# The first chunk of a gated recurrence: whole loads of k, q and v, f by halves of heads, one more transpose by DMA, and a new order of the program

## The chip, the cores and the metric

The kernel runs on one core of a Trainium2 chip. The metric is device time in microseconds for one launch. Three runs of the kernel before took 181.29, 182.45 and 182.78 us; the median, 182.45 us, is the time to compare with.

## What is computed

The reference is a linear recurrence with a gate for each key channel, followed by a two-layer network with a leaky ReLU. There are 4 batches, 8 heads, 768 tokens and 48 channels for each head; the network is 384 to 2048 to 384.

```python
f = 1.0 / (1.0 + np.exp(-f_logit))
for t in range(S):
    state = f[:, :, t, :, None] * state + np.einsum('bhd,bhe->bhde', k[:, :, t], v[:, :, t])
    y[:, :, t] = np.einsum('bhd,bhde->bhe', q[:, :, t], state)
x = y.transpose(0, 2, 1, 3).reshape(B * S, H * D)
h = x @ w_in
out = np.maximum(0.01 * h, h) @ w_out
```

## The kernel before, in words

**Units.** The 768 tokens are cut into 6 chunks of 128. One chunk of one batch is a unit: 24 units, numbered so that units 0 to 3 are the first chunk of the four batches (the first quad), 4 to 7 the second chunk, and so on. Two neighbouring units are a pair `m`.

**A unit from the second chunk on.** f, k, q and v are loaded with tokens on partitions (`load_part`, L171, 192 KB each, runs of 192 B). ScalarE makes log(1 + exp(-f)) (`gate_exp`, `gate_ln`), TensorE sums it over tokens with a triangular matrix (`gate_pe`, L328), and ScalarE makes the decays from it (`decay_em`, `decay_a`). `k_scale` and `q_scale` multiply k and q by them. They are turned, so that channels lie on partitions, by TensorE (`turn_pe`) or for a pair at once by DMA (`turn2_dma`, L376). `score_pe` makes the scores, `mask` cuts them to the lower triangle, `mix_pe` (L418) makes the 128x384 result from the scores and the state, and `state_pe`, `state_dve`, `state_pool` carry the state on. `y_out` puts the result into SBUF as bf16, and it is turned once more for the network: by TensorE (`x_pe`, L453, three transposes, and `x_out`), or for a pair by one DMA on SP's queue (`x2_dma`, L380), for the pairs that the tuple `X2` (L200) lists.

**The network.** `up` (L462) makes two of the 16 blocks of hidden channels for a pair, 6 products of 256 columns; `up_act` is its leaky ReLU on ScalarE. `down` (L484) is one half of the second layer for a unit, 8 products of 384 columns. `put` and `out_dma` store the result. A pair has 8 `up`; units 4 and 5 have forms of their own for one unit (`up1`). The weights are loaded and cast to bf16 by DMAs of GpSimd's queue: `load_w_in` in two halves (half 0 serves groups 0 to 3 of `up`, half 1 groups 4 to 7), `load_w_out` in four parts.

**The first quad** has a form of its own (functions with `q_`), since all four units start from a state of zero. f of all four is loaded into one tile `fq` with 32 partitions for each batch, each holding four neighbouring tokens, so that a run is 768 B; k and q (`kq`, `qq`) likewise, but with the batches interleaved on the partitions. One ScalarE instruction then handles half of the heads of all four units (`q_exp_act`, L228, and `q_ln_act`, L231). `q_gate32` (L234) makes the sums over tokens for half of the heads into four banks, one for each batch; `q_decay_b` (L243) makes the decays of a batch, for half of the heads or all, positive sign (`emT`) or negative (`aT`). `q_k_cast`, `q_q_cast` make bf16 of k and q, `q_turn_pe` turns them, `q_mul` (L260) multiplies by the decays. Then come `q_score_pe`, the mask (`q_mask` on VectorE, or an eviction by ScalarE, `q_wf_act`, with `q_mask_pool` on GpSimd), `q_back_pe` and `q_back_out` (k turned back for the state), `state_pe`, `q_mix_pe`, `y_out`, `x_pe` and `x_out`. v of units 0 to 3 comes by four `load_part` and four `cast_v`.

**The order.** Nothing is scheduled by the compiler. The program is a list written out call by call (from L513), and each engine and each DMA queue runs its part of the list in that order; waits follow from which tile or bank is read and written. So a wait of one engine holds back all that stands behind it on that engine. SP's queue issues the loads, stores and transposing DMAs, and holds back everything behind a DMA whose data is not ready. `touch` (L183) is a small copy on GpSimd that waits for a load and so delays the weight loads behind it on the queue. `idle_pe` (L140) issues dummy products on TensorE.

Of the kernel before, what the change touches and what calls it, by code (L numbers as in the profile page):

```python
# [9 lines left out]
FP32 = mybir.dt.float32  # L10
# [6 lines left out]
def kernel(  # L17
# [50 lines left out]
    def load_quad(eng, t, src, b, h):  # L68
        rows = slice(32 * b, 32 * b + 32) if t is fq else slice(b, None, 4)
        eng.dma_start(out=t[rows, h, :, :].rearrange("p h j d -> p h (j d)"),  # L70
                      in_=src[b, h, 0:C, :].rearrange("h (t j) d -> t h (j d)", j=4))

    quads = {"f": (fq, f_logit), "k": (kq, k), "q": (qq, q)}

    def first_load(eng, name, b, hh=None):
        load_quad(eng, quads[name][0], quads[name][1], b, slice(0, H) if hh is None else slice(4 * hh, 4 * hh + 4))
# [7 lines left out]
    first_load(nc.sync, "k", 1)  # L84
    first_load(nc.sync, "k", 2)
    first_load(nc.sync, "k", 3)
    first_load(nc.sync, "q", 0)
    first_load(nc.sync, "q", 1)
    first_load(nc.sync, "q", 2)
    first_load(nc.sync, "q", 3)  # L90
# [80 lines left out]
    def load_part(u, name, src):  # L171
        c, b = units[u]
        t = raws[f"{name}_raw"][u % R_RAW]
        nc.sync.dma_start(out=t, in_=src[b, :, c * C:(c + 1) * C, :].rearrange("h t d -> t h d"))
        raw.setdefault(u, {})[name] = t
# [24 lines left out]
    X2 = (9, 10, 11)  # L200
# [23 lines left out]
    emT, aT = wide(gTs[GBUFS - 1]), wide(gTs[GBUFS - 2])  # L224
    kTq = [const.tile([128, 2, 4, 128], BF16, name=f"kTq{i}", tag=f"kTq{i}") for i in range(2)]
# [287 lines left out]
    q_exp_act(0)  # L513
    q_ln_act(0)
    load_part(0, "v", v)
    q_exp_act(1)
    load_part(1, "v", v)
    idle_pe(24, 7)
    q_gate32(0, 0, 1, 2, 3)
    touch('k')  # L520
    q_k_cast(V, 0)
    q_ln_act(1)
    q_k_cast(G, 1)
    q_turn_pe(khq, 0, 4)
    load_part(2, "v", v)
    q_decay_b(0, aT, -1.0, 0, 0)
    q_gate32(1, 0, 1, 2, 3)
    q_decay_b(1, emT, 1.0, 1, 0)
    load_w_in(0)
    q_decay_b(0, emT, 1.0, 0, 0)  # L530
    q_decay_b(2, emT, 1.0, 2, 0)
    q_turn_pe(khq, 1, 5)
    q_k_mul(0, 1, 0, 4)
    q_decay_b(1, aT, -1.0, 1, 0)
    load_w_in(1)
    q_decay_b(2, aT, -1.0, 2, 1)
    q_k_mul(0, 0, 0, 4)
    q_decay_b(1, emT, 1.0, 1, 1)
    load_part(3, "v", v)
    q_q_cast(V, 1)  # L540
    q_decay_b(3, emT, 1.0, 3, 1)
    q_decay_b(0, emT, 1.0, 0, 1)
    q_q_cast(V, 0)
    idle_pe(6, 7)
    q_turn_pe(qhq, 1, 6)
    q_decay_b(0, aT, -1.0, 0, 1)
    load_part(4, "f", f_logit)
    cast_v(G, 0)
    q_decay_b(1, aT, -1.0, 1, 1)
    q_k_mul(1, 0, 0, 5)  # L550
    q_turn_pe(qhq, 0, 7)
    q_decay_b(2, aT, -1.0, 2, 0)
    q_k_mul(1, 1, 0, 5)
    q_decay_b(2, emT, 1.0, 2, 1)
    q_q_mul(1, 0, 0, 6)
    q_decay_b(3, aT, -1.0, 3, 1)
    cast_v(G, 1)
    idle_pe(1, 1)
    q_back_pe(1, 0)
    q_q_mul(1, 1, 0, 6)  # L560
    q_decay_b(3, aT, -1.0, 3, 0)
    q_back_pe(0, 1)
    q_q_mul(0, 0, 0, 7)
    q_decay_b(3, emT, 1.0, 3, 0)
    q_back_out(A, 0, 1)
    q_q_mul(0, 1, 0, 7)
    idle_pe(2, 2)
    q_score_pe(1, 0, 2, 3)
    q_back_out(V, 1, 0)
    q_q_mul(1, 0, 1, 6)  # L570
    q_score_pe(0, 0, 1, 0)
    q_wf_act(1, 0, 1, 3)
    q_mask(1, 0, 0, 2)
    state_pe(1, 3)
    q_wf_act(0, 0, 1, 0)
    q_mask_pool(1, 0, 1)
    q_mask(0, 0, 0, 1)
    state_pe(0, 2)
    q_state_dve(0)
    q_mask_pool(0, 0, 1)  # L580
    q_k_mul(0, 0, 1, 4)
    q_mix_pe(1, 0)
    q_state_pool(0)
    load_part(4, "k", k)
    q_mix_pe(0, 1)
    q_k_mul(1, 0, 1, 5)
    y_out(A, 1, 0)
    q_state_dve(1)
    y_out(A, 0, 1)
    idle_pe(3, 2)  # L590
    x_pe(1, 2)
    q_k_mul(1, 1, 1, 5)
    x_pe(0, 0)
    q_state_pool(1)
    x_out(A, 1, 2)
    q_q_mul(0, 1, 1, 7)
    x_out(A, 0, 0)
    q_q_mul(1, 1, 1, 6)
    q_q_mul(0, 0, 1, 7)
    idle_pe(5, 1)  # L600
    q_score_pe(1, 1, 1, 3)
    q_k_mul(0, 1, 1, 4)
    up(0, 2, 5)
    q_mask(1, 1, 0, 1)
    q_wf_act(1, 1, 1, 3)
    q_back_pe(3, 2)
    up(0, 1, 6)
    up_act(0, 2, 5)
    q_mask_pool(1, 1, 1)
    q_back_out(V, 3, 2)  # L610
    up(0, 0, 0)
    up_act(0, 1, 6)
    q_score_pe(0, 1, 7, 4)
    up_act(0, 0, 0)
    up(0, 3, 3)
    q_mask(0, 1, 0, 7)
    q_wf_act(0, 1, 1, 4)
    load_part(4, "q", q)
    cast_v(G, 2)
    q_back_pe(2, 1)  # L620
    up_act(0, 3, 3)
    load_w_out(0)
    q_back_out(V, 2, 1)
    idle_pe(1, 0)
    up(0, 4, 5)
    load_part(4, "v", v)
    cast_v(V, 3)
    q_mask_pool(0, 1, 1)
    state_pe(2, 2)
    up(0, 5, 6)  # L630
    up_act(0, 4, 5)
    load_w_out(1)
# [756 lines left out]
```

## Time and profile before

| quantity | value |
|---|---|
| median of three runs | 182.45 us |
| the profiled execution | 182.43 us, span 180.7 us |
| TensorE busy | 171.3 us, 95% of the span |
| ScalarE busy | 123.4 us, 68% |
| VectorE busy | 87.0 us, 48% |
| GpSimd busy | 54.8 us, 30% |
| DMA moved | 31.31 MB, mean 173 GB/s |
| last product ends, last eviction ends | 177.50 us, 177.85 us |

PE in the profile is TensorE's matrix product, PEld its loading of the stationary operand (which overlaps), DVE is VectorE, ACT ScalarE, POOL GpSimd, SP SyncE. Times in a timeline are from the start of the span: start, length, engine, line of the kernel, operation, output and input, count, and in brackets how long the engine stood idle before it and who ended the wait. Helpers hide the caller: `move` (L148, L150) stands for all copies. The matrix unit can be called busy while its clock is halved; the column PEclk of the table by stretches shows the granted clock.

### The profile page before, as it was taken

How to read it: one execution, taken by the hardware profiler on the slowest of the kernel's cores; microseconds unless marked ns; L12 is line 12 of the kernel's file. 1: busy time of each engine (PE TensorE's matmuls, PEld its weight loads, DVE VectorE, ACT ScalarE, POOL GpSimd, SP SyncE). 2: the span in 40 equal slices, each digit the busy share in tenths (PEclk: the TensorE clock that was granted, in tenths of full speed). 3: DMA queues.
4: the chain of work that ended last, by engine and by line, in shares of the span. 5: the costliest groups of instructions: out<-in, count | busy, mean ns of one | idle time of the engine just before them, and what ended most of it. 6: DMA issues, size and time to landing. Idle time of an engine off the chain costs nothing.

```text
span 180.7 us, 4845 instructions
## 1 busy us (share of the span) xinstructions
PE 171.3 (95%) x1912; PEld 137.7 (76%) x1912; DVE 87.0 (48%) x203; ACT 123.4 (68%) x268; POOL 54.8 (30%) x108
## 2 busy tenths in 40 slices
PE   7597899999999999979999999999999999999992
PEld 5375699776788889669778788788785696897872
DVE  7249954044765978176467365670750254100000
ACT  2577689546888998758779669578796382583711
POOL 3074453114455646330421804250532300000000
PEclk9969999999999999999999999999999999999999
DMA  5999999979988999999999999998999962050102
GB/s 151 303 221 192 211 173 228 210 157 202 219 188 180 193 173 199 169 209 254 163 192 218 185 206 144 249 186 172 234 207 205 201 180 44 5 131 0 44 25 109
DMA packets 112582, 31.31 MB, mean 173 GB/s; under 512 B 105008, under 2 KB 111280, under 8 KB 112560
## 3 DMA queue, kind: packets, MB, share of 16 engines
q1 hardware_dynamic: 110640, 27.47, 79.7%
q0 software_dynamic: 1376, 3.15, 9.5%
q10 hardware_dynamic: 544, 0.39, 0.8%
q8 instruction: 15, 0.25, 0.6%
q14 instruction: 7, 0.06, 0.1%
HBM read 25.17 MB, written 4.72 MB: 165 GB/s over the span
## 4 chain that ended last, share of the span: by engine, by line
PE 54%; ACT 0%; issue 0%
PE ps L466 24%; PE ps L486 22%; PE ps L404 2%; PE ps L425 2%; PE ps L491 1%; PE ps L422 1%; PE ps L332 1%; PE ps L456 1%; PE ps L433 1%; PE ps L335 0%; ACT osb L148 0%
## 5 line engine op out<-in xcount | busy, mean ns | idle before, releaser
L486 PE MATMUL ps<-w_out_b,gT 128*128 128x384 bf16 x368 | 65.9, 326 | 0.0
L466 PE MATMUL ps<-xT,w_in 128*128 128x256 bf16 x528 | 64.5, 273 | 1.0 <-DVE xT L150 1.0
L471 ACT ACTIVATE gT<-ps 128x512 bf16<-128x512 f32 x88 | 51.7, 601 | 15.0 <-PE ps L466 12.9
L466 PEld LDWEIGHTS <-w_in 128*128 128x128 bf16 x528 | 56.0, 114 | 3.0 <-issue 1.1
L486 PEld LDWEIGHTS <-gT 128*128 128x128 bf16 x368 | 34.5, 98 | 19.8
L415 DVE TENSOR_TENSOR wm<-ps,ut 128x512 bf16<-128x512 f32 x40 | 25.2, 683 | 13.2 <-PE ps L404 11.6
L148 ACT COPY osb<-ps 128x384 f32<-128x384 f32 (+1 forms) x24 | 11.2, 466 | 21.2 <-PE ps L486 17.3
L316 POOL CAST sb<-sf 64x192 bf16<-64x192 f32 x40 | 14.6, 364 | 22.4 <-PE ps L422 18.9
L358 POOL TENSOR_TENSOR kqh<-q_raw,a_t 128x384 bf16<-128x384 f32 x11 | 10.1, 920 | 20.1 <-ACT a_end L344 6.8
L150 DVE CAST xn<-ps 128x384 bf16<-128x384 f32 x15 | 8.3, 556 | 7.6 <-PE ps L425 4.5
L354 POOL TENSOR_TENSOR kqh<-k_raw,em_t 128x384 bf16<-128x384 f32 x7 | 6.4, 918 | 17.6 <-ACT em_t L339 13.3
L354 DVE TENSOR_TENSOR kqh<-k_raw,em_t 128x384 bf16<-128x384 f32 x13 | 8.6, 658 | 6.6 <-ACT em_t L339 6.3
L339 ACT ACTIVATE em_t<-ps 128x384 bf16<-128x384 f32 x20 | 10.0, 498 | 2.0 <-PE ps L335 1.9
L323 ACT ACTIVATE f_raw<-f_raw 128x384 f32<-128x384 f32 x20 | 10.6, 530 | 1.0 <-DMA f_raw<-in_f_logit_dram 1.0
L150 POOL CAST v_b<-v_raw 128x384 bf16<-128x384 f32 x11 | 6.5, 588 | 15.8 <-DMA v_raw<-in_v_dram 15.8
L326 ACT ACTIVATE lf<-f_raw 128x384 bf16<-128x384 f32 x20 | 10.5, 526 | 0.3
L142 PE MATMUL ps<-fill 128*128 128x256 bf16 x46 | 9.3, 364 | 1.3 <-DVE fill L107 1.3
L342 ACT ACTIVATE a_t<-ps 128x384 bf16<-128x384 f32 x20 | 9.9, 495 | 0.8 <-PE ps L335 0.5
L358 DVE TENSOR_TENSOR kqh<-q_raw,a_t 128x384 bf16<-128x384 f32 x9 | 5.8, 644 | 7.2 <-ACT a_t L342 6.8
L150 DVE CAST v_b<-v_raw 128x384 bf16<-128x384 f32 x13 | 6.5, 503 | 5.3 <-DMA v_raw<-in_v_dram 5.2
L447 POOL TENSOR_TENSOR sf<-sf,a_end 128x192 f32<-128x192 f32 x16 | 8.8, 549 | 0.4
L441 DVE TENSOR_TENSOR sf<-sf,ps 64x192 f32<-64x192 f32 x16 | 5.5, 343 | 5.2 <-PE ps L433 1.8
(83 smaller groups left out, 192.6 us busy)
## 6 DMA issues: line engine op xcount, KB each, us to landing
v_raw<-in_v_dram SPq DMA_DIRECT2D x24, 192.0 KB, 4.4
out_dram<-osb SPq DMA_DIRECT2D x23, 192.0 KB, 3.2
f_raw<-in_f_logit_dram SPq DMA_DIRECT2D x20, 192.0 KB, 4.3
k_raw<-in_k_dram SPq DMA_DIRECT2D x20, 192.0 KB, 4.3
q_raw<-in_q_dram SPq DMA_DIRECT2D x20, 192.0 KB, 4.4
w_in<-in_moe_w_in_dram POOLq DMA_DIRECT2D x2, 768.0 KB, 10.8
w_out_b<-in_moe_w_out_dram POOLq DMA_DIRECT2D x4, 384.0 KB, 6.7
kq<-in_k_dram SPq DMA_DIRECT2D x4, 192.0 KB, 4.8
```

Source lines behind the costliest of these rows:

```text
L148: eng.copy(out=out, in_=in_)
L150: eng.tensor_copy(out=out, in_=in_)
L316: nc.gpsimd.tensor_copy(out=state_b[b][r, :, e * D:(e + 1) * D], in_=state_f[b][r])
L323: nc.scalar.activation(raw[u]["f"], raw[u]["f"], AF.Exp, scale=-1.0)
L326: nc.scalar.activation(lfs[u % R_LF][:, :, 0:D], raw[u]["f"], AF.Ln, bias=1.0)
L339: nc.scalar.activation(em_ts[u % R_EM], bank(bk)[:, 0:H * D], AF.Exp, scale=1.0)
L354: eng.tensor_mul(khs[u % R_KQS][:, :, 0:D], raw[u]["k"], em_ts[u % R_EM])
L358: eng.tensor_mul(qhs[u % R_KQS][:, :, 0:D], r["q"], a_ts[u % R_EM])
L415: nc.vector.tensor_mul(wms[e][u % R_WM], bank(bk).rearrange("p (i n) -> p i n", i=P2), ut[:, None, :].to_broadcast([128, P2, 128]))
L466: nc.tensor.matmul(bank(bk)[:, i * 256:(i + 1) * 256].rearrange("p (a n) -> p a n", a=2), w_in_p[ff // 8][:, kk, ff // 4 % 2, :, ff % 4], ...
L471: nc.scalar.activation(gTs[m % GBUFS][:, 2 * g:2 * g + 2].rearrange("p f a n -> p (f a n)"), bank(bk), AF.Prelu, alpha=0.01)
L486: nc.tensor.matmul(bank(bk)[:, 0:KD], g_part(u)[:, ff, :], w_out_b[:, ff, :], start=(ff == 0), stop=(ff == NF - 1))
```

## The change

- f of the first quad is loaded in eight DMAs, the first half of the heads of all four batches ahead of the second half; four on SP's queue, four on ScalarE's.
- k, q and v of the first quad are loaded by one DMA each (`load_all`), with the layout that k and q had. v gets that layout too. It lies in `vq`, and is cast to bf16 as `vqb` by `q_v_cast`. TensorE then puts the tokens of a batch on partitions: `q_pick` multiplies by a selection matrix `pick` (four products of 384 columns for each unit), and `q_v_out` evicts the result as `v_b`. The matrix is set up once, by GpSimd and VectorE. The three tiles lie in buffers of the network that are not in use yet.
- `touch` waits for q instead of k, so that the weights are loaded after q; the second half of `w_in` is now loaded first.
- x of units 16 and 17 (pair 8) is turned by DMA: `X2` is (8, 9, 10, 11).
- The list of calls is new as a whole. Exp and ln of unit 4 now stand among the evictions of the first quad; all four units of the quad stand ahead of the first `up`, but for some products of 2 and 3; the dummy products are placed anew (42 instead of 46); the pairs' `up` and `down` come in another order, as do loads, stores and the choice of engine for copies.

The diff, without most of the new list:

```diff
+    def load_all(t, src):
+        nc.sync.dma_start(out=t.rearrange("p h j d -> p h (j d)"),
+                          in_=src[:, :, 0:C, :].rearrange("b h (t j) d -> t b h (j d)", j=4))
-    first_load(nc.scalar, "f", 2)
-    first_load(nc.sync, "f", 0)
-    first_load(nc.sync, "f", 1)
-    first_load(nc.scalar, "f", 3)
-    first_load(nc.sync, "k", 0)
...
-    first_load(nc.sync, "q", 3)
+    first_load(nc.scalar, "f", 2, 0)
+    first_load(nc.sync, "f", 0, 0)
+    first_load(nc.sync, "f", 1, 0)
+    first_load(nc.scalar, "f", 3, 0)
+    first_load(nc.sync, "f", 0, 1)
+    first_load(nc.scalar, "f", 2, 1)
+    first_load(nc.sync, "f", 1, 1)
+    first_load(nc.scalar, "f", 3, 1)
+    load_all(kq, k)
     nc.scalar.preload_act_table_set("natural_log_exp_and_others")
+    load_all(qq, q)
-    X2 = (9, 10, 11)
+    X2 = (8, 9, 10, 11)
+    pick = spare[:, 0:2048].rearrange("p (b i t j) -> p b i t j", b=B, i=4, j=4)
+    nc.gpsimd.memset(pick, 0.0)
+    for i in range(4):
+        nc.vector.tensor_copy(out=pick[:, :, i, :, i], in_=ident.rearrange("p (t b) -> p b t", b=B))
+    def q_v_cast(eng, hh):
+        move(eng, vqb[:, 4 * hh:4 * hh + 4], vq[:, 4 * hh:4 * hh + 4])
+    def q_pick(b, bk):
+        for i in range(4):
+            nc.tensor.matmul(bank(bk)[:, 0:H * D].rearrange("p (h d) -> p h d", h=H),
+                             pick[:, b, i].rearrange("p t j -> p (t j)"), vqb[:, :, i, :], start=(i == 0), stop=(i == 3))
+    def q_v_out(eng, b, bk):
+        move(eng, v_bs[b].rearrange("p h d -> p (h d)"), bank(bk)[:, 0:H * D])
```

The new list up to the first `up`, by engine (calls of one engine in their order; a number ahead of `x` counts equal calls):

```
SyncE    f 0 and 1 (two halves each), k, q, v; then load_part 4 f, k, q, v; 5 f
ScalarE  q_exp_act 0, q_ln_act 0, q_exp_act 1, q_ln_act 1,
         q_decay_b: aT of 0 (half); gate products of half 1 follow it; then aT 1, emT 1, emT 0, aT 1, emT 1, emT 0 (halves), emT 3, emT 2 (whole),
         q_q_cast 1, aT 2 (whole), aT 0 (half), q_back_out 1, q_back_out 0, aT 3 (whole), q_wf_act 0 0, q_wf_act 1 0,
         q_v_out 1, gate_exp 4, q_v_out 2, gate_ln 4, q_v_out 0, q_wf_act 1 1, q_back_out 3, y_out 1, q_wf_act 0 1,
         y_out 0, decay_a 4, x_out 1, x_out 0
VectorE  q_k_cast 0, 3 x q_k_mul, q_q_cast 0, 3 x q_k_mul, 4 x q_q_mul, q_v_cast 0, q_k_mul, 4 x q_q_mul, q_k_mul,
         q_mask 0 0, q_mask 1 0, q_state_dve 1, q_mask 1 1, q_back_out 2, q_mask 0 1, q_state_dve 0, q_state_dve 2
TensorE  24 x dummy, q_gate32 0, 5 x dummy, q_gate32 1, q_turn_pe k 0, k 1, 9 x dummy, q_turn_pe q 0, q_back_pe 1, q_turn_pe q 1,
         q_back_pe 0, dummy, q_score_pe 0 0, 1 0, q_pick 1, 2, 0, state_pe 1, q_score_pe 1 1, q_back_pe 3, q_score_pe 0 1,
         q_mix_pe 1, state_pe 0, q_back_pe 2, gate_pe 4, q_mix_pe 0, q_pick 3, x_pe 1, state_pe 2, x_pe 0, dummy, q_mix_pe 2, dummy, up(0, 6)
GpSimd   q_k_cast 1, touch q, load_w_in 1, load_w_in 0, q_v_cast 1, q_mask_pool 0 0, 1 0, 1 1, q_state_pool 1, q_mask_pool 0 1, load_w_out 1, 0
```

Behind it on TensorE stand `q_mix_pe(3)`, `state_pe(3)`, `x_pe(2)`, `up(0, 5)`, `up(0, 7)`, `x_pe(3)`, `up(0, 4)`, one dummy and the `up` of pair 1. Further on, around the place at 78 us, the new list has:

```diff
+    cast_v(V, 12)
...
+    x_out(V, 8, 5)
...
+    k_scale(V, 12)
...
+    x_out(V, 9, 0)
...
+    up(4, 7, 1)
```

and for pair 8 `y_out(A, 16, 0)`, `load_part(21, "f", f_logit)`, `x2_dma(8)`, five `up` of pair 7 and three `down`, then `up(8, 0, 5)`.

More of the change, by code (lines that the diff above doesn't have):

```diff
@@ L603 @@
[L603 to L626, printed above, removed]
@@ new lines @@
+    q_v_out(A, 2, 7)
+    state_pe(1, 6)
+    gate_ln(4)
+    q_score_pe(1, 1, 1, 5)
+    q_mask(1, 0, 0, 2)
+    q_v_out(A, 0, 3)
+    q_back_pe(3, 4)
+    q_score_pe(0, 1, 7, 0)
+    q_state_dve(1)
+    q_wf_act(1, 1, 1, 5)
+    q_mix_pe(1, 2)
+    q_back_out(A, 3, 4)
+    state_pe(0, 3)
+    q_mask(1, 1, 0, 1)
+    q_back_pe(2, 5)
+    q_mask_pool(1, 1, 1)
+    gate_pe(4, 6)
+    y_out(A, 1, 2)
+    q_mix_pe(0, 4)
+    q_back_out(V, 2, 5)
+    q_wf_act(0, 1, 1, 0)
+    q_state_pool(1)
+    q_pick(3, 1)
@@ L1167 @@
[L1167 to L1172 removed]
+    score1_pe(4, 2, 6)
+    gate_ln(6)
+    load_part(7, "q", q)
+    put(V, 3, 3)
+    turn_pe(5, 5)
+    mask(4, 0, 2)
+    down(0, 1, 4)
+    turn_q(A, 5, 5)
+    load_part(7, "v", v)
+    turn_k(V, 5, 5)
+    mask(4, 1, 6)
+    gate_pe(6, 7)
+    load_part(8, "f", f_logit)
+    score1_pe(5, 0, 3)
+    put(A, 0, 4)
+    cast_v(V, 6)
+    decay_em(6, 7)
+    mix_pe(4, 2)
+    mask(5, 1, 3)
@@ new lines @@
+    decay_a(6, 7)
+    down(1, 1, 1)
+    load_part(8, "k", k)
+    k_scale(G, 6)
+    y_out(A, 4, 2)
+    mask(5, 0, 0)
+    gate_exp(7)
+    q_scale(G, 6)
+    load_part(8, "q", q)
+    state_pe(5, 5)
+    gate_ln(7)
+    x_pe(4, 6)
+    put(V, 1, 1)
+    state_pe(6, 4)
+    mix_pe(5, 7)
+    x_out(A, 4, 6)
+    state_pool(4)
+    state_dve(5)
+    gate_pe(7, 3)
+    load_part(8, "v", v)
+    turn_pe(6, 2)
+    y_out(A, 5, 7)
+    state_dve(6)
+    decay_em(7, 3)
+    up1(4, 2, 0)
+    decay_a(7, 3)
```

1447 lines of the change are left out of this document (695 added, 752 removed).

## The prediction

> **What bounds the kernel now.** I read the page's head first (busy time, and TensorE's busy tenths in 40 slices of 4.5 us), then TensorE's own waits, and last the start of the timeline engine by engine.
>
> ```profile
> span 180.7 us, 4845 instructions
> ...
> PE 171.3 (95%) x1912; PEld 137.7 (76%) x1912; DVE 87.0 (48%) x203; ACT 123.4 (68%) x268; POOL 54.8 (30%) x108
> ...
> PE   7597899999999999979999999999999999999992
> ```
>
> TensorE's waits from 30 us on, the whole list:
>
> ```profile
> PE ps L466 <- DVE xT L150: 1.0, 1, 1.0
> ```
>
> So TensorE is the bound from the sixth slice on (22.6 us), with one hole of 1.0 us in the eighteenth (near 78 us). Before that it is busy in part only, and in part with dummy products. The end of the kernel is therefore set by three things: when TensorE starts on the dense work (the first `up`), how much useful work is left then, and what holes come later. The tail (last eviction, last store) is the same in both kernels, and I leave it out.
>
> Here is what sets the start now, ScalarE first, then TensorE:
>
> ```profile
> 6.44 0.84 ACT L229 ACTIVATE fq<-fq 128x768 f32<-128x768 f32 x1 [3.39 <-DMA fq<-in_f_logit_dram]
> ...
> 8.92 0.84 ACT L232 ACTIVATE lfq<-fq 128x768 bf16<-128x768 f32 x1
> 9.67 0.37 ACT L245 ACTIVATE gT<-ps 128x256 f32<-128x256 f32 x1
> ...
> 11.16 4.25 ACT L245 ACTIVATE gT<-ps 128x256 f32<-128x256 f32 x15 [1.12 <-PE ps L240]
> 15.14 0.75 ACT L148 COPY kqh<-ps 128x512 bf16<-128x512 bf16 x1
> 15.88 1.10 ACT L281 CAST wm<-ps 128x512 bf16<-128x512 f32 x2
> 18.20 0.86 ACT L148 CAST xn<-ps 128x384 bf16<-128x384 f32 x2 [1.22 <-PE ps L294]
> 19.11 0.86 ACT L148 COPY xT<-ps 128x384 bf16<-128x384 bf16 x2
> ```
>
> ```profile
> 8.21 0.63 PE L240 MATMUL ps<-steps,lfq 32*128 32x128 bf16 x32 [1.74 <-ACT lfq L232]
> ...
> 10.09 1.04 PE L240 MATMUL ps<-steps,lfq 32*128 32x128 bf16 x32
> ...
> 20.98 0.74 PE L466 MATMUL ps<-xT,w_in 128*128 128x256 bf16 x5
> ```
>
> The load of f ends at 6.44; exp and ln of both halves take until 9.76; the gate products of the second half end at 11.13; from there ScalarE's evictions and decays lead, by way of VectorE, to x of units 0 and 1 at 19.97, and the first `up` runs at 20.98.
>
> **The change, part by part.** The sum is made against the profiled execution (182.43 us, span 180.7); the median of the runs is 182.45, the same.
>
> *f in halves.* Four loads become eight of half the size. By these rows the first 393 KB have moved by 3.7 us (151 KB by 3.0, 506 by 4.0), and all 786 KB by 5.0:
>
> ```profile
> 2.00:3.00 1.00, 1.00 (x7) 0.69 (x6) 0.96 (x9) 1.00 (x1) 0.38 (x3) 1.00 0.68 151
> 3.00:4.00 1.00, 1.00 (x6) 0.69 (x5) 0.97 (x10) 0.05 (x1) 0.00 (x0) 1.00 1.07 355
> 4.00:5.00 1.00, 1.00 (x6) 0.74 (x5) 1.00 (x8) 0.00 (x0) 0.00 (x0) 1.00 1.11 290
> ...
> 10.00:11.00 1.00, 0.94 (x33) 0.82 (x32) 0.00 (x0) 0.04 (x1) 1.00 (x3) 0.50 1.32 239
> ```
>
> Exp starts 1.4 after the last byte now, so I let the first half's exp start at 5.1. The ends are 4.4 (the shortest landing in the row below, 3.6 after an issue at 0.8) and 6.44 (no gain). Exp and ln take 3.3 in all as before, so ln of half 1 ends at 8.4.
>
> ```profile
> DMA to landing us min/median/max: 3.6/4.1/5.0
> ```
>
> Issues and landings of q's four loads, for comparison (columns of the first row: least, median and longest issue in ns, first and last issue in us):
>
> ```profile
> L70 SPq DMA_DIRECT2D qq<-in_q_dram x4: 599/606/612, 4.6 to 6.9; - x4
> ...
> DMA to landing us min/median/max: 4.1/4.3/4.5
> ```
>
> The two extra issues on each queue cost at most 0.6 each. They push k's issue and, on ScalarE's queue, the load of the activation table back by up to 1.2; both have until f has landed.
>
> The first decay (0.37) comes ahead of the second gate products and reads the bank that they write, so they start at 8.8. They took 1.04 at a granted clock of 0.50 and the first set 0.63; I take 0.85, which puts their end at 9.7 instead of 11.13. The Trainium skill (TensorE: Matmul & The Clock Gate, Part 1) says that the clock falls to half after an idle window of about 3.4 us; the 0.50 row, after TensorE's pause of 1.74, agrees in kind. The changed order leaves a pause of some 0.4 in that place, so by the rule alone the clock would stay full and the sum below would be 0.2 lower.
>
> *ScalarE from 9.7 to the first `up`.* Ahead of it in ScalarE's new order stand: 7 half decays (4.25 / 15 = 0.28 each, 2.0), 4 whole decays and 4 score evictions of 128x512 (1.10 / 2 = 0.55 each, 4.4), 3 `q_back_out` (0.6 each, between 0.55 and 0.75; 1.8), one cast of q (0.84), 3 `q_v_out`, 2 `y_out` and 2 `x_out` (0.43 each, 3.0), and exp, ln and the decay of unit 4 (about 0.5 each, 1.5). The sum is 13.5, with no wait, so the first `up` runs at 23.2. The check against now: from 11.16 to 19.97 ScalarE has 7.8 of such work and 1.2 of waiting. Every piece is of a kind that the rows above price. Does another engine end later? By the rows below VectorE has, from the first k decays, out at 10.6, to the last mask, 16 products (1.41 / 4 = 0.35), 4 masks (1.27 / 2 = 0.64), a state update (0.73) and three casts or evictions, which I price like a mask: 10.8 in all, to 21.4. That leaves 1.8, and a VectorE late by less is covered.
>
> ```profile
> 14.18 1.41 DVE L263 TENSOR_TENSOR qTq<-ps,gT 128x256 bf16<-128x256 bf16 x4
> ...
> 16.17 1.27 DVE L288 TENSOR_TENSOR wm<-ps,ut 128x512 bf16<-128x512 f32 x2
> 17.36 0.73 DVE L310 TENSOR_TENSOR sf<-ps,gT 64x192 f32<-64x192 f32 x2
> ...
> 77.55 1.03 DVE L150 CAST v_b<-v_raw 128x384 bf16<-128x384 f32 x1 [1.61 <-DMA v_raw<-in_v_dram]
> ```
>
> That is +2.2 (23.2 for 20.98). The bounds are 22.3 (f at 4.4 and a full clock) and 24.7 (f at 6.44, half clock).
>
> *What no longer follows the first `up`.* Prices by the chain of work in the dense part:
>
> ```profile
> 80.00 1.31 PE ps L466 x12
> 81.31 0.55 PE ps L404 x16
> ...
> 85.43 0.20 PE ps L425 x8
> ...
> 86.01 0.17 PE ps L332
> 86.17 0.08 PE ps L335 x4
> 86.25 1.32 PE ps L486 x8
> 87.57 0.34 PE ps L456 x6
> ...
> 89.86 0.17 PE ps L433 x4
> ```
>
> Before, these follow the first `up`: `q_score_pe(0, 1)` (half of 0.55), `q_back_pe` of 3 and 2 (8 transposes, 0.45), state, mix and x of 2 and 3 (0.34, 0.40, 0.34) and `gate_pe(4)` (0.25), 2.05. After, only mix, state and x of 3, and x of 2: 0.71. That is -1.34. Dummy products behind that point fall from 5 to 1, at 0.11 each: -0.44. The products of `q_pick` are 16 of 128x384, 2.6 in all by the 1.32 row. They lie ahead of the first `up`, while TensorE waits for ScalarE; if that cover failed, they would cost up to 2.6.
>
> *K, q, v by one load each.* Twelve issues become three and the bytes stay. k was waited for as a whole already, by one cast. q is wanted by its cast at 12.5 and lands at 11.4 or earlier (issued up to 6.9, and 4.5). v comes in runs of 768 B instead of 192 B and should land 2.4 behind q, by 13.8 (786 KB at the 320 GB/s that the rows of 355 and 290 make); `q_v_cast` wants it at 14.9. Nothing of it is on the path. I give it zero, with 0 to +0.6 as ends (one more issue as in the row of f, and a margin of 1.1 that could shrink).
>
> *x of 16 and 17 by DMA.* Six transposes leave TensorE, -0.34, with their evictions. SP gets one more transposing DMA, which waits for `y_out` of 16; behind it stand the loads of units 21 and on. Between that DMA and the first `up` of pair 8 stand 5 `up` and 3 half `down`, 7.2 us of TensorE by the rows above, which is the cover. Ends: -0.34 and, as the one hole that SP's lateness has made here shows, +1.0.
>
> *The hole at 78.* It came from a cast of v (13) that waited 1.61 for its load and stood ahead of the x eviction that `up` needed. In the new order that x eviction stands behind the cast of v (12), which is four loads earlier in SP's order. I take 0.2 for the new hole, between 0 and 1.04: -0.84.
>
> *Sum:* 2.2 - 1.34 - 0.44 - 0.34 - 0.84 = -0.76, which gives **181.7**. With the bounds of the start alone it runs from 180.8 to 183.2; with the hole as well, from 180.6 to 184.0.
>
> **The rivals.** *f of unit 4 comes late: slower.* `gate_exp(4)` stood behind the seventh `up`. Now it stands among ScalarE's evictions, with 7.8 of work ahead of it from 9.7, so its turn is at 17.5, and behind it stand all evictions that lead to x. Its load stands behind v's on SP's queue. What it meets are the weights, which now wait for q instead of k. With q at 11.1 to 11.4 and half a microsecond for the copy that waits, they are issued at 11.6 to 11.9 and move from 12.0 on; before, they were issued at 9.99 and the loads' rate fell at once (239 in the row of 10 to 11 us):
>
> ```profile
> 9.99 1.73 POOL L190 DMA_DIRECT2D w_in<-in_moe_w_in_dram  x2
> ```
>
> ```profile
> 12.13 0.50 POOL L150 CAST v_b<-v_raw 128x384 bf16<-128x384 f32 x1 [0.41 <-DMA v_raw<-in_v_dram]
> ...
> 13.21 0.69 POOL L150 CAST v_b<-v_raw 128x384 bf16<-128x384 f32 x1 [0.58 <-DMA v_raw<-in_v_dram]
> ```
>
> ```profile
> L174 SPq DMA_DIRECT2D v_raw<-in_v_dram x4: 580/732/1864, 7.6 to 10.8; - x4
> ...
> DMA to landing us min/median/max: 4.5/7.0/13.2
> ```
>
> At 12.0 some 330 KB stand ahead of f's end: f's 197 and the last 0.4 us of v. In the kernel before, at 10.0, at most 393 KB (v of 0 and 1) stood there and had landed by 13.2, 3.2 later; that speaks against this rival and gives a landing at 15.2. But the last v of the four landed at 24.0 (10.8 + 13.2), 10.8 after the second: two loads of 197 KB in 10.8 us, 36 GB/s. At that rate from the start f takes 9.2 and lands at 21.2, 3.7 late, which gives **185.4**. It decides from a landing at 17.5 on. The Trainium skill (DMA: Bandwidth & Descriptors, Queues, rings and completion order) says that a DMA engine takes turns between its queues by packets; by that rule small packets beside the weights' large ones get little, which is this rival. The 36 GB/s agree, the 3.2 us do not.
>
> *The start packs tighter: faster.* If f's half lands at 4.4, the clock stays full and no later hole comes, the first `up` is at 22.3: 1.3 - 1.34 - 0.44 - 0.34 - 1.04 = -1.86, **180.6**. For it speaks that ScalarE's pieces are all plain; against it, that the sum knows no wait at all.
>
> *The weights come late.* The first `up` now needs the load of `w_in` that is issued first, at 11.6 or a little later. The two took 9.1 and 12.5:
>
> ```profile
> DMA to landing us min/median/max: 9.1/10.8/12.5
> ```
>
> They land at 20.7 or 24.1; the second is 0.9 behind the first `up` and gives **182.6**.
>
> **How the numbers follow.** The forecast has 0.46, the late f 0.16, the tight start 0.26 (the same sum at its low ends), the late weights 0.12. The range is 180.0 to 184.8: below, the tight start with half a microsecond for pieces that overlap more than the sum lets them; above, most of the late f. A measurement here can tell about 1%, 1.8 us. Below 180.6 lie two thirds of the tight start (0.17) and the lower edge of the forecast (0.08): 0.25. Above 184.3 lie most of the late f (0.12) and the upper edge of the late weights and of the forecast, with a large new hole (0.06): 0.18. The rest, 0.57, is the same.
>
> **What would show it.** Right: exp of the first half of f near 5.1, the second gate products over by 9.7, ScalarE without a wait from there, the first `up` near 23.2, TensorE then without holes over 0.2. Wrong: a wait of ScalarE for `f_raw` at exp of unit 4, TensorE waiting for the weights at the first `up`, holes behind casts of v, or `q_pick` after TensorE became the bound.

## The result and the profile after

The median of 20 runs is 182.12 us (180.90 to 183.37), beside 181.83 us (181.29 to 183.28) of 20 runs of the kernel before on the same chip. The ratio is 1.0006, with a 95% interval of 0.9987 to 1.0026: no change that can be told. The profiled execution took 182.57 us (span 180.9), where that of the kernel before took 182.43.

The head of the page of the changed kernel: span, busy time, and TensorE's busy tenths in slices of 4.5 us.

```profile
span 180.9 us, 4820 instructions
...
PE 171.8 (95%) x1918; PEld 138.5 (77%) x1918; DVE 87.1 (48%) x206; ACT 124.3 (69%) x268; POOL 56.3 (31%) x106
...
PE   7758999999999999999999999999999999999993
```

The eighteenth slice is full now: the hole at 78 us is gone. TensorE's longest wait now lies ahead of the first `up`. From the list of TensorE's waits (us in total, times, longest):

```profile
PE ps L276 <- DVE khq L147: 2.4, 1, 2.4
...
PE ps L484 <- ACT xT L145: 0.3, 1, 0.3
PE ps L350 <- ACT lf L344: 0.3, 1, 0.3
```

The second and third are the only ones behind 24 us. The first is `q_turn_pe`, waiting for the bf16 of K. VectorE's cast of K, in the changed kernel and in the kernel before:

```profile
10.36 0.56 DVE L147 CAST khq<-kq 128x768 bf16<-128x768 f32 x1 [2.54 <-DMA kq<-in_k_dram]
```

```profile
8.68 0.56 DVE L150 CAST khq<-kq 128x768 bf16<-128x768 f32 x1 [3.17 <-DMA kq<-in_k_dram]
```

The timeline of TensorE in the changed kernel:

```profile
7.96 0.63 PE L247 MATMUL ps<-steps,lfq 32*128 32x128 bf16 x32 [0.64 <-ACT gT L252]
10.97 1.52 PE L276 MATMUL ps<-ident,khq 128*128 128x128 bf16 x16 [2.38 <-DVE khq L147]
12.29 2.12 PE L139 MATMUL ps<-fill 128*128 128x256 bf16 x9
...
24.71 0.81 PE L484 MATMUL ps<-xT,w_in 128*128 128x256 bf16 x6 [0.34 <-ACT xT L145]
...
176.42 1.48 PE L509 MATMUL ps<-w_out_b,gT 128*128 128x192 bf16 x16
```

The gate products of the second half end at 8.6, which is 1.1 earlier than forecast and 2.5 earlier than before. Then TensorE stands still until K is there. The first `up` runs at 24.71, 3.73 later than in the kernel before, and from it to the end of the last product TensorE takes 153.19 us (before: 156.52). The two differences nearly cancel.

ScalarE in the same stretch, with three waits that the sum did not have:

```profile
4.27 0.84 ACT L236 ACTIVATE fq<-fq 128x768 f32<-128x768 f32 x1 [0.28 <-DMA fq<-in_f_logit_dram]
...
12.74 0.83 ACT L145 CAST qhq<-qq 128x768 bf16<-128x768 f32 x1 [1.38 <-DMA qq<-in_q_dram]
...
15.61 1.26 ACT L145 COPY kqh<-ps 128x512 bf16<-128x512 bf16 x2 [1.27 <-PE ps L318]
...
19.16 0.48 ACT L145 CAST v_b<-ps 128x384 bf16<-128x384 f32 x1 [0.73 <-PE ps L266]
19.53 0.53 ACT L341 ACTIVATE f_raw<-f_raw 128x384 f32<-128x384 f32 x1
```

The last row is the exp of unit 4. It did not wait for its f.

The issues on SP's queue, and three stretches (the last three columns are the granted clock, the DMA share and GB/s):

```profile
3.45 0.71 SPq L74 DMA_DIRECT2D kq<-in_k_dram  x1
4.21 0.66 SPq L74 DMA_DIRECT2D qq<-in_q_dram  x1
4.91 2.27 SPq L74 DMA_DIRECT2D gT<-in_v_dram  x1
```

```profile
5.00:6.00 1.00, 0.90 (x8) 0.51 (x6) 1.00 (x11) 0.97 (x3) 0.00 (x0) 1.00 0.46 78
6.00:7.00 1.00, 0.95 (x36) 0.82 (x37) 1.00 (x6) 0.97 (x2) 0.00 (x0) 1.00 0.80 223
...
13.00:14.00 1.00, 1.00 (x7) 0.67 (x5) 1.00 (x4) 1.00 (x3) 1.00 (x2) 0.50 1.20 242
```

Two things stand there. The DMA engines run half empty at 5 to 6 us: f is through and K, issued at 3.45 only, has hardly begun. And the granted clock is 0.50 from 12 us, after the pause.

### The profile page after: what moved, and what is told of

The parts are those of the page before. It is cut to its first block, busy times and chain, and to the rows that moved or that the text cites. A ratio compares the mean times of both kernels' runs of the same rounds, so it can differ in the third digit from the quotient of the medians.

```text
span 180.9 us, 4820 instructions
## 1 busy us (share of the span) xinstructions
PE 171.8 (95%) x1918; PEld 138.5 (77%) x1918; DVE 87.1 (48%) x206; ACT 124.3 (69%) x268; POOL 56.3 (31%) x106
## 4 chain that ended last, share of the span: by engine, by line
PE 83%; DMA 5%; DVE 4%; ACT 4%; issue 1%; POOL 1%; DVEq 0%
PE ps L504 32%; PE ps L484 31%; DMA kq<-in_k_dram 4%; PE ps L495 3%; PE ps L422 2%; PE ps L443 2%; PE ps L440 2%; PE ps L350 2%; DVE qTq L281 2%; PE ps L509 1%; DMA fq<-in_f_logit_dram 1%; PE ps L451 1%; PE ps L474 1%; PE ps L139 1%; PE ps L385 1%; PE ps L276 1%
## 5 line engine op out<-in xcount | busy, mean ns | idle before, releaser
L504 PE MATMUL ps<-w_out_b,gT 128*128 128x384 bf16 x368 | 65.0, 326 | 0.0
L484 PE MATMUL ps<-xT,w_in 128*128 128x256 bf16 x528 | 63.2, 273 | 0.3 <-ACT xT L145 0.3
L145 ACT COPY osb<-ps 128x384 f32<-128x384 f32 (+1 forms) x22 | 10.2, 465 | 28.9 <-PE ps L504 26.1
L376 POOL TENSOR_TENSOR kqh<-q_raw,a_t 128x384 bf16<-128x384 f32 x13 | 12.7, 979 | 19.2 <-ACT a_t L360 7.7
L372 DVE TENSOR_TENSOR kqh<-k_raw,em_t 128x384 bf16<-128x384 f32 x13 | 7.7, 589 | 15.6 <-ACT em_t L357 15.5
L357 ACT ACTIVATE em_t<-ps 128x384 bf16<-128x384 f32 x20 | 10.2, 510 | 4.3 <-PE ps L353 3.4
L372 POOL TENSOR_TENSOR kqh<-k_raw,em_t 128x384 bf16<-128x384 f32 x7 | 7.1, 1010 | 15.5 <-DMA k_raw<-in_k_dram 8.9
L147 DVE CAST xn<-ps 128x384 bf16<-128x384 f32 x12 | 6.5, 556 | 9.0 <-PE ps L443 7.3
L139 PE MATMUL ps<-fill 128*128 128x256 bf16 x42 | 8.6, 366 | 1.3 <-DVE fill L104 1.3
L147 POOL CAST v_b<-v_raw 128x384 bf16<-128x384 f32 x5 | 2.7, 543 | 15.9 <-DMA v_raw<-in_v_dram 15.8
L139 PEld LDWEIGHTS <-fill 128*128 128x128 bf16 x42 | 5.3, 131 | 3.0 <-DVE fill L104 1.3
```

Source lines behind the costliest of these rows:

```text
L139: nc.tensor.matmul(bank(bk)[:, 0:256], fill[:, 0:128], fill[:, 0:256], start=True, stop=True)
L145: eng.copy(out=out, in_=in_)
L147: eng.tensor_copy(out=out, in_=in_)
L372: eng.tensor_mul(khs[u % R_KQS][:, :, 0:D], raw[u]["k"], em_ts[u % R_EM])
L376: eng.tensor_mul(qhs[u % R_KQS][:, :, 0:D], r["q"], a_ts[u % R_EM])
L484: nc.tensor.matmul(bank(bk)[:, i * 256:(i + 1) * 256].rearrange("p (a n) -> p a n", a=2), w_in_p[ff // 8][:, kk, ff // 4 % 2, :, ff % 4], ...
```

## The experiments

Theory A was: the eight pieces of f push K's one load back, so K, q and v land late, and what the early f wins is lost again. The program's loads on SP and ScalarE share eight completion semaphores in turn, so the ninth load, K, waits until the first piece of f is in (in the first profile its last part signals at 3.43). From the changed kernel's list of waits on SP's queue:

```profile
SPq L74 <- DMA fq<-in_f_logit_dram: 0.8, 1, 0.8
```

Rivals were that one load of 768 KB is late by itself (B), that the start does not set the end (C), and later that the granted clock is the cause (F). The table gathers the profiles; all versions have the new order, except where the kernel before is named. The experiments ran on four chips, on which the kernel before had a median of 181.42 us (e1 to e4), 181.33 (e5 to e8), 181.36 (e9 to e11) and 181.49 (e12); the ratios below are to the kernel before on the same chip, and they compare better than the medians.

| version | K issued | K's cast starts | 0.50 clock after 9 us | first `up` | first `up` to end of last product | median of runs |
|---|---|---|---|---|---|---|
| changed kernel | 3.45 | 10.36 | yes | 24.71 | 153.19 | 182.12 |
| e1, the same program | 3.55 | 10.04 | yes | 23.94 | 153.20 | 181.44 |
| e6, changed kernel again | 3.50 | 9.67 | no | 22.55 | 153.20 | 181.41 |
| e2, K by four loads | 3.47 | 9.54 | no | 23.15 | 153.20 | 182.11 |
| e3, f whole | 1.75 | 8.26 | yes | 23.43 | 153.19 | 181.60 |
| e5, K by GpSimd's queue | 1.34 | 9.38 | yes | 26.30 | 153.20 | 183.70 |
| e8, x of 16 and 17 on TensorE | 3.61 | 10.08 | no | 23.00 | 153.54 | 181.62 |
| e9, gap filled | 3.54 | 10.79 | no | 23.73 | 153.20 | 181.48 |
| e10, f whole, gap filled | 1.75 | 9.48 | no | 22.78 | 153.20 | 181.25 |
| e12, K eighth | 2.20 | 10.17 | yes | 24.30 | 153.20 | 181.90 |
| before | | 8.68 | yes | 20.98 | 156.52 | 181.83 |
| e7, before again | | 8.51 | yes | 20.94 | 155.30 | (one run, 181.19) |
| e11, before filled | | 8.38 | no | 20.50 | 155.31 | 180.96 |

Behind the first `up` every version of the new order in the table takes the same 153.20 us to 0.01, but for e8, which has six transposes more: there TensorE is the bound, and theory C falls. All that varies is the start.

**e1, K's call ahead of the last piece of f.**

```diff
+    load_all(kq, k)
     first_load(nc.scalar, "f", 3, 1)
-    load_all(kq, k)
```

> One call is moved: the load of k stands ahead of the last of f's eight loads, so that it is the eighth load and not the ninth. Theory A (a load waits until the load eight places before it has landed, so f's eight loads hold k back by 0.8 us, the transfers run dry at 5 to 6 us, and k's landing at 10.3 sets the start): k is issued at 2.7 instead of 3.45 and lands near 9.6, the first k product is 0.7 earlier (11.0 instead of 11.7), and the first up is 0.5 to 0.7 earlier (24.0 to 24.2 instead of 24.7). The time falls by 0.3% against the changed kernel. Rival B (one large load lands late because its slowest part does, whatever its issue): k lands at 10.0 or later, the first up stays at 24.5 or later. Rival C (the start is held by ScalarE, by v or by the weights, not by k): k lands earlier and the first up stays within 0.2 of 24.7.

181.44 us, ratio 1.0002 (0.9987 to 1.0018). The last piece of f goes by ScalarE's queue, so neither queue's order changed, and K was issued at 3.55 as before: this is the changed kernel once more, and it says nothing on A. It shows that the first `up` moves between executions of one program (23.94, 24.71).

**e2, K by four loads of 192 KB.**

```diff
-    load_all(kq, k)
+    for b in range(B):
+        nc.sync.dma_start(out=kq[slice(b, None, 4)].rearrange("p h j d -> p h (j d)"),
+                          in_=k[b, :, 0:C, :].rearrange("h (t j) d -> t h (j d)", j=4))
```

> k alone is loaded by four loads again, one for each batch, behind f's eight; q and v stay whole. Theory A: the four are issued from 3.45 to about 5.5 and the last lands 4.8 behind its issue, so k is there at 10.1 to 10.5, as now (10.3), and the first up stays within 0.4 of 24.7. Rival B (the large load itself is slow to land): f and k together have moved by 8.1 us, so four loads land by 9.2, and the first k product comes before 10.9.

182.11 us, ratio 1.0036 (1.0018 to 1.0055). Each quarter landed 3.2 to 3.9 us after its issue, where one load takes 6.2 to 7.2 in the order of the changed kernel. But the three further issues moved q's to 6.2 and v's to 6.9; K's cast came at 9.54, and TensorE then waited for q. Four loads win little for K and lose it on q and v.

**e3, f by four whole loads.**

```diff
-    first_load(nc.scalar, "f", 2, 0)
...
-    first_load(nc.scalar, "f", 3, 1)
+    first_load(nc.scalar, "f", 2)
+    first_load(nc.sync, "f", 0)
+    first_load(nc.sync, "f", 1)
+    first_load(nc.scalar, "f", 3)
```

> f is loaded by four loads of all heads again; everything else is as in the changed kernel. Theory A: k is the fifth load, waits for nothing, is issued at 1.8 and lands near 8.7, q near 11 and v near 14.5; the first exp falls back from 4.3 to 6.4 and ln of the second half ends at 9.8 instead of 7.6; the first up stays within 0.7 of 24.7, since what f gave k took away. Rival D (the halves of f are worth their 2.1 us at the first up, and the late k costs little): the first up is at 26 or later and the time 1% above that of the changed kernel.

181.60 us, ratio 1.0013 (1.0001 to 1.0026). K's issue and TensorE in this version:

```profile
1.75 0.73 SPq L74 DMA_DIRECT2D kq<-in_k_dram  x1
```

```profile
9.87 1.04 PE L243 MATMUL ps<-steps,lfq 32*128 32x128 bf16 x32 [0.60 <-ACT gT L248]
10.85 1.89 PE L272 MATMUL ps<-ident,khq 128*128 128x128 bf16 x16
...
23.43 0.81 PE L480 MATMUL ps<-xT,w_in 128*128 128x256 bf16 x6 [0.34 <-ACT xT L141]
```

The exp of f starts 2.0 later than in the changed kernel, and the first `up` is inside the changed kernel's own spread. So f in halves buys nothing that reaches the first `up`. K, issued 1.7 earlier, is cast at 8.26 (9.48 in e10, with the same loads), and its transposes follow the gate products of the second half without a wait: what TensorE waits for last ahead of them is f here, and not K.

**e4, v by four loads and casts, as before.**

```diff
...
-    load_all(vq, v)
+    load_part(1, "v", v)
...
+    load_part(3, "v", v)
...
-    q_pick(1, 5)
...
-    q_v_out(A, 1, 5)
+    cast_v(G, 1)
...
```

The same is done for the other three units, and `q_v_cast` and the setting up of `pick` are left out.

> v of units 0 to 3 comes by four loads with tokens on partitions and four casts again, without the selecting products and their evictions; everything else is as in the changed kernel. Theory A: k and q still set the start, so the first up moves by less than the 1.6 us of evictions that ScalarE sheds, to 23.7 to 24.5, unless the small runs of v make it land later than now (16.6 for all four); the time stays within 0.5% of the changed kernel. Rival E (the new way of v costs the 2.6 us of products and 1.6 us of evictions in full): the first up is before 23.3 and the time 0.8% lower. Rival F (small runs of v crawl beside the weights, as two of them did in the kernel before, landing at 18 and 24): units 2 and 0 or 3 wait for v, and the first up is at 25.5 or later.

189.93 us median of four runs: three took 189.64 to 190.33, one 183.53. The profile is of one of the three. Exp of unit 4, SP's issues, and TensorE's longest wait:

```profile
25.76 0.52 ACT L337 ACTIVATE f_raw<-f_raw 128x384 f32<-128x384 f32 x1 [9.10 <-DMA f_raw<-in_f_logit_dram]
```

```profile
4.99 8.55 SPq L171 DMA_DIRECT2D v_raw<-in_v_dram  x4
13.58 0.81 SPq L171 DMA_DIRECT2D f_raw<-in_f_logit_dram  x1
```

```profile
PE ps L314 <- ACT wm L295: 8.0, 1, 8.0
```

(No trace shows the run of 183.53 us.) This is my slower rival, larger than its 185.4: v's four loads hold SP's queue until 13.54, f of unit 4 gets in behind the weights, lands 12.2 after its issue, and all evictions behind its exp wait. In the changed kernel the same load is issued at 7.22, lands at 17.2, and is wanted at 19.5. The one load of v is what keeps this rival away. The Trainium skill (DMA: Bandwidth & Descriptors, Queues, rings and completion order) has the DMA engines take turns between queues; f's 12.2 us beside the weights of GpSimd's queue agree with it.

**e5, K by GpSimd's queue.**

```diff
-    load_all(kq, k)
+    load_all(kq, k, nc.gpsimd)
```

`load_all` gets the issuing engine as a third argument.

> The changed kernel with its one load of K issued on GpSimd's queue, ahead of GpSimd's other work, instead of on SP; nothing else. K then waits for none of the eight completion counters of the SP and ScalarE queues, and q takes its place as the ninth load there. Theory A (K is late because it is issued at 3.45 us behind a wait of 0.8 us and the transfers run dry at 5 to 6 us): K is issued by 2.5 us and lands by 9.2 us rather than 10.0 to 10.4, q lands by 11.5, ScalarE's waits for q and for the turned K shrink below 1 us together, the first up product comes at 22.5 to 23.3 us rather than 23.9 to 24.7, and the time is 0.8 to 1.4 us under that of the changed kernel in the same call. Theory B (one load of 768 KB lands late because the last of its parts is late, whenever it is issued): K lands at 9.8 us or later and the time is within 0.4 us of the changed kernel. Theory C (the start does not set the end): the first up product comes earlier, but the time stays within 0.4 us, because the wait returns later in the program.

183.70 us, ratio 1.0117 (1.0090 to 1.0145), against A's forecast. K was issued at 1.34 and still landed at 9.4, 8.0 later, and it took the DMA engines from f:

```profile
9.94 0.84 ACT L236 ACTIVATE fq<-fq 128x768 f32<-128x768 f32 x1 [3.94 <-DMA fq<-in_f_logit_dram]
```

The second half of f came 4 us later than in the changed kernel, and the granted clock was 0.50 from 10.4 to 17.3. Here K got ahead of f only at f's cost.

**e6, the changed kernel again; e7, the kernel before again.**

> The changed kernel once more, for the spread and as the partner of the others of this call. Theory A: the first up product again at 23.9 to 24.8 us, time 181.3 to 182.2 us, ratio to the kernel before 0.999 to 1.003. If the first profile was an odd execution: the first up product at 23.2 us (what my sum had) and the time 0.5 us or more under the kernel before.

> The kernel before, profiled once more. My sum counted 0.84 us for TensorE's hole at 78 us, which the first profile of this kernel showed (1.04 us, behind a cast of v that waited for its load). If the hole belongs to the kernel: a wait of 0.8 to 1.2 us at 77 to 80 us again, first up at about 21.0. If it belonged to that one execution (182.43 us, 0.6 us over the median of its 20 runs): no wait over 0.4 us there, and a span of 179.6 to 180.2 us instead of 180.7.

e6: 181.41 us (12 runs), ratio 0.9996 (0.9977 to 1.0014). VectorE's cast of K and TensorE in e6:

```profile
9.67 0.56 DVE L147 CAST khq<-kq 128x768 bf16<-128x768 f32 x1 [1.83 <-DMA kq<-in_k_dram]
```

```profile
10.29 1.30 PE L276 MATMUL ps<-ident,khq 128*128 128x128 bf16 x16 [1.67 <-DVE khq L147]
11.43 1.15 PE L139 MATMUL ps<-fill 128*128 128x256 bf16 x9
...
22.55 0.82 PE L484 MATMUL ps<-xT,w_in 128*128 128x256 bf16 x6 [0.34 <-ACT xT L145]
```

K was cast 0.69 earlier than in the first profile, and the first `up` came 2.16 earlier. The other 1.47 is the clock: the same nine dummies take 1.15 here and 2.12 there. From K's cast to the first `up` it is 12.88 us here and 12.92 and 12.94 in e8 and e9, where the clock stayed full too; with the clock at half it is 13.90 in e1 and 14.35 in the first profile. (In e2, also at full clock, it is 13.61, because q came later there, at 12.4.)

e7: 181.19 us, and behind 22 us TensorE waits for nothing at all. The hole at 78 us, 0.84 of my sum, belonged to that one execution of the kernel before; e11, with its 155.31, has none either.

**e8, x of 16 and 17 on TensorE.**

```diff
-    X2 = (8, 9, 10, 11)
+    X2 = (9, 10, 11)
...
+    x_pe(17, 3)
...
-    x2_dma(8)
+    x_out(V, 17, 3)
+    x_pe(16, 0)
+    x_out(A, 16, 0)
```

> The changed kernel with x of units 16 and 17 turned on TensorE again (two times 3 transposes, two copies out of PSUM on VectorE and ScalarE) in place of the one transpose by DMA; the rest of the order as it is. My sum priced this part at 0.34 us of TensorE's time: the time is then 0.2 to 0.5 us over the changed kernel of the same call. Rival: TensorE has small waits there that hide the transposes, or the queue behind the DMA transpose gains what TensorE loses, and the time is within 0.15 us of the changed kernel or under it.

181.62 us beside e6's 181.41; the ratios to the kernel before, 1.0020 (0.9999 to 1.0041) and 0.9996 (0.9977 to 1.0014), overlap, so the times alone don't settle it. The profile does: behind the first `up` it is 153.54 instead of 153.20, which is the 0.34 of the sum.

**e9, e10, e11: dummy products in the pause.**

```diff
     q_gate32(1, 0, 1, 2, 3)
+    idle_pe(14, 7)
```

In e10 (the changed kernel with f whole, as in e3) and e11 (the kernel before) `idle_pe(36, 7)` stands in place of `idle_pe(24, 7)` ahead of the first gate products.

> The changed kernel with 14 dummy products (1.5 us at full clock) behind the second gate products, in TensorE's pause before K's transposes; nothing else. Theory F (the executions of the changed kernel differ because K's landing moves that pause between 1.7 and 2.4 us, and in the longer case the granted clock falls to 0.50 for some 3 us from 11 or 12 us on, which the chain to the first up product crosses): no rows of 0.50 after 10 us in any profile, K's transposes in 1.3 us rather than 1.5 to 1.7, the first up product at 22.4 to 23.3 us, and a median 0.4 to 0.9 us under that of the changed kernel (181.4 and 182.1 us in two calls), with less spread. Theory G (the landings of K, q and v alone set the first up product and the clock only follows): the clock stays full, but the first up product is spread over 22.5 to 24.5 us as before and the median is within 0.3 us of the changed kernel. A third way: the dummies end after K's cast and delay its transposes, the first up product at 23.5 us or later.

> The changed kernel with f by four whole loads and 36 dummy products in place of 24 ahead of the first gate products, where this version's TensorE had waited 1.72 us and the granted clock had then been 0.50 from 9.4 to 12.7 us. Theory F: the clock stays full, the second gate products take 0.63 instead of 1.04 us and K's transposes 1.3 instead of 1.9, the first up product comes at 22.3 to 22.8 us instead of 23.43, and the time is 0.5 to 1.1 us under the 181.6 us of the version without the dummies. Theory G: the first up product stays within 0.3 us of 23.43. The third way: the dummies run at half rate until after f has landed and delay the first gate products, the first up product after 23.7 us.

> The kernel before with 36 dummy products in place of 24 ahead of the first gate products; nothing else. It asks whether the kernel before pays for its pause of 1.7 us at 6.5 to 8.2 us too (granted clock 0.50 from 10 to 13 us in both of its profiles). Theory F: the clock stays full, the second gate products take 0.63 instead of 1.04 us, the first up product comes at 20.0 to 20.5 us instead of 20.9 to 21.0, and the time is 0.4 to 1.0 us under the kernel before. Theory G: first up and time within 0.3 us of the kernel before.

e9: 181.48 us, ratio 1.0011 (0.9985 to 1.0036); e10: 181.25, 0.9985 (0.9967 to 1.0003); e11: 180.96, 0.9988 (0.9970 to 1.0005). In all three profiles the clock stays full (e9's trace has no record of the clock; its products run at full rate, nine dummies in 1.15 us). e9's rows:

```profile
10.79 0.56 DVE L147 CAST khq<-kq 128x768 bf16<-128x768 f32 x1 [2.96 <-DMA kq<-in_k_dram]
```

```profile
8.79 1.70 PE L139 MATMUL ps<-fill 128*128 128x256 bf16 x14
11.41 1.30 PE L276 MATMUL ps<-ident,khq 128*128 128x128 bf16 x16 [0.92 <-DVE khq L147]
...
23.73 0.81 PE L484 MATMUL ps<-xT,w_in 128*128 128x256 bf16 x6 [0.34 <-ACT xT L145]
```

The dummies ended 0.30 before K's cast and 0.92 before its transposes, so they delayed nothing; K had landed later than in any other profile. Theory F is right on the stretch between K's cast and the first `up` (1.0 to 1.5 us less than at half clock) and wrong on the first `up` itself, at 23.73, and on the median, which did not move, as theory G has it. e10 and e11 gained 0.65 and 0.44 us at the first `up`, and stand 0.12 to 0.15% under the kernel before, which their intervals don't tell from nothing.

The mean granted clock of every run shows how often the clock falls. It is 0.991 in the first profile, with one stretch at 0.50, and 1.000 in e6. Of the first 20 runs of the changed kernel 17 are at 0.991 or under (median 182.18 us, the other three 181.27), of e6's 12 it is seven (181.45 and 180.89). With the gap filled it is two of 12 in e9 and none of 12 in e10, where e3 has ten of ten. So the dummies do keep the clock up. But the ten runs of e9 at full clock have a median of 181.38, beside 181.36 of the kernel before on that chip. In the profiled one of them K was late, with its cast at 10.79; of the others no trace tells. In e10, where K is not what TensorE waits for, the ratio is 0.28% under that of e3, at the edge of what the two intervals can tell.

**e12, K as the eighth load.**

```diff
-    first_load(nc.sync, "f", 1, 1)
...
     make_identity(nc, ident)
+    first_load(nc.gpsimd, "f", 1, 1)
```

> The changed kernel with one of f's eight half loads (unit 1, second half) issued on GpSimd's queue, behind the making of the identity matrix; nothing else. K's load is then the eighth on the SP and ScalarE queues and waits for no completion counter, and K stays behind the other seven pieces of f. In two executions of the changed kernel's order in which the clock stayed full (the second profile of the changed kernel and the one with the gap filled), the first up product came 12.88 us after the start of K's cast, both times. Theory A (the eight pieces of f cost K its place): K is issued at 2.2 to 2.4 us instead of 3.45 to 3.55, lands at 8.4 to 9.3, its cast starts by 9.3, the first up product comes at 21.4 to 22.3 us and the time is 179.4 to 180.3 us, 1.0 us or more under both kernels. Theory B (one load of 768 KB is late whenever it is issued): K lands at 9.7 or later, the first up product at 22.5 us or later, time as the changed kernel's. Theory D (K takes the DMA engines from f, as when K went by GpSimd's queue): the exp of the second half waits over 0.8 us for the last piece of f, and the first up product comes 15 us behind that exp, at 22.3 us or later.

(The cast of e9, for which this text counts 12.88 us as well, gives 12.94 by its row above.) 181.90 us, ratio 1.0019 (0.9995 to 1.0043). SP, GpSimd, ScalarE:

```profile
2.20 0.73 SPq L74 DMA_DIRECT2D kq<-in_k_dram  x1
```

```profile
2.35 0.74 POOL L70 DMA_DIRECT2D fq<-in_f_logit_dram  x1
```

```profile
8.75 0.84 ACT L236 ACTIVATE fq<-fq 128x768 f32<-128x768 f32 x1 [2.80 <-DMA fq<-in_f_logit_dram]
```

Theory D. The piece of f on GpSimd's queue took 6.4 us beside K, where the other seven took 2.5 to 4.3; and K, issued 1.25 earlier and without a wait, landed at 10.2, after 8.0 us. So the wait for the semaphore alone isn't what makes K late, and A in that form falls. (B's numbers are met as well: K at 10.2, the first `up` at 24.30, and the time of the changed kernel.)

What remains of K's lateness can be counted. Summed over 1 us rows, 2.23 MB had moved when K was cast in the first profile of the changed kernel (2.0 to 10.36), and 1.85 MB in e3 (2.0 to 8.26); f and K are 1.57 MB. So 0.65 and 0.27 MB of the loads behind it had moved when K was in. The traces also hold the moments at which the parts of one load signal that they are done; K has 16. In e3 all 16 signals lie between 7.67 and 8.24. In the first profile of the changed kernel eleven lie between 8.33 and 8.91, and the last five follow at 9.29, 9.34, 9.68, 9.79 and 10.33. So of the 2.1 us between the two, about 0.7 are a later arrival of K as a whole (from 4 to 7 us 360 KB less moved, 515 against 874), and 1.4 are a few parts that lag behind the others. The Trainium skill (DMA: Bandwidth & Descriptors, Why a DMA increments its semaphore by 16 and not by 1) says that the up to 16 engines of one load finish independently and that only the last of them counts; the 16 signals agree. This is what theory B says, and it holds in every version with one load of K but e3: the 16 signals lie 1.6 to 2.6 us apart from first to last, in e10 too (7.36 to 9.46), where f is whole. Why some parts lag, and why by a microsecond more or less between executions, stays open. That q and v issued later would help K was not tried.

## Why the prediction was right, and where it was not

It was right in time, in part by luck. The sum started from 182.45 us for the kernel before, of which 20 runs have a median of 181.83, 0.6 less; and it forecast a change of -0.76, where the medians differ by +0.29, 1.05 more. The two errors have opposite signs and leave 182.12 for 181.7.

*f in halves:* right in mechanism, and better than forecast (exp at 4.27 for 5.1, gate products over at 8.6 for 9.7), but not what sets the first `up`: e3.

*"K, q, v by one load each ... Nothing of it is on the path. I give it zero":* this is the step that failed. I let K land in time because it "was waited for as a whole already", and priced it as if a load of four times the size, issued behind twice as many, would land when the bytes have moved. It landed at 10.36, later by 1.7 than in the kernel before (8.68). K then set TensorE, q landed at 12.7 where the prediction had 11.4 at the latest, ScalarE waited 1.38 for it, and the first `up` came at 24.71 for 23.2. Over the executions of this order it lies at 22.55 to 24.71, -0.65 to +1.5 against the forecast.

*The clock:* I took 0.85 for the second gate products as a mean of both clocks and let it end there. The pause moved: 0.64 at most ahead of the gate products, a new one of 1.67 to 2.38 us ahead of K's transposes, which costs 1.0 to 1.5 us when the clock falls. "By the rule alone the clock would stay full" named the wrong pause.

*Less work, fewer dummies, x by DMA:* -1.34 - 0.44 - 0.34 = -2.12 forecast; 153.20 - 155.30 = -2.10 measured against the hole-free profile.

*The hole at 78:* -0.84 forecast, and so it was between the first two profiles (-1.22 with what hung on it). e7 and e11 have no hole, so in such a run there was nothing to win. I took one execution's wait for the kernel's.

Together, against a run without the hole: about -2.1 of work, and a start later by 1.6 to 3.7. That puts the changed kernel between 0.5 us under and 1.6 us over the kernel before; the ratio of 1.0006 lies between.

*Rivals:* f of unit 4 was in time, but e4 shows the mechanism, so its chance was not idle. The weights made no wait at the first `up` in any profile. The tight start came in one profiled execution of the changed kernel (e6, 22.55 and 180.43 us), not in the median.

## What to carry to other kernels

When a gating load is split or moved forward, price the load that is waited for next with its own issue and landing, not with the bytes: here f came 2 us earlier, and the first `up` then waited for K. A wait seen in one execution should be looked for in a second one before a gain is counted on it. And dense work behind a fixed start can be priced to hundredths of a microsecond, so the effort belongs to the start.

## What the runs showed of the hardware

One program's start moves by over 2 us between executions, and most of that is an amplifier: K 0.69 later made the pause 2.38 instead of 1.67, the clock fell to 0.50, and the first `up` was 2.16 later. No length of the pause alone decides it: 1.65 (e7), 1.72 (e3) and 1.94 (e1) were followed by a clock of 0.50, 1.67 (e6), 1.77 (e4) and 1.85 (e8) were not.

What the traces show is a grid in time. In every profile whose trace recorded the clock (all but e9), each later change of the clock lies a whole multiple of 3.41 us after the first one, the rise to full clock near the start; in the first profile of the changed kernel the dummies start every 0.21 us until then, and every 0.11 us from then on. The rise comes at another moment in each execution of one program: at 5.07 in the first profile of the changed kernel, at 6.39 in e6. So the pause before K's transposes lies on the grid in different ways. Here are one stretch of the first profile (TensorE's busy time is the first number behind the length) and two of e6:

```profile
8.48:11.90 3.42, 0.97 (x21) 0.70 (x14) 0.75 (x2) 2.75 (x8) 1.21 (x1) 1.00 1.09 338
```

```profile
6.39:9.80 3.41, 1.99 (x70) 1.40 (x69) 1.58 (x10) 2.67 (x8) 0.10 (x1) 1.00 1.06 342
9.80:13.22 3.42, 2.77 (x35) 2.24 (x36) 2.63 (x8) 2.76 (x7) 2.25 (x3) 1.00 1.11 318
```

In the first profile the whole pause fell into one stretch of the grid, TensorE stood idle for 2.45 of 3.42 us, and the clock was 0.50 from 11.90 on, for one such length. In e6 the pause was split, with 1.42 and 0.65 idle, and the clock stayed full. How much idle time a stretch takes is not settled: e3 lost the clock after a stretch with 1.72, e4 kept it after 1.77 and lost it after 1.35. The Trainium skill (TensorE: Matmul & The Clock Gate, Part 1) says that the activity window runs freely and isn't tied to the kernel's start, so that the moment of the change differs from run to run; the grid agrees with that, and its 3.41 us with the idle window of about 3.4 us that the prediction cites from there. That a window has to be idle does not fit as it stands: here stretches that were about half idle were enough.

One load of 768 KB landed 6.2 to 8.0 us after its issue as K, 6.2 to 9.3 as q behind it, and 8.6 to 11.7 as v behind both; one of 192 KB, a quarter of K in e2, landed after 3.2 to 3.9. Issued at 1.34 or 2.20, among f's pieces, K took the 8.0.
